# A tau-masked attention with a gated feed-forward layer on one core: weight pieces of 512 columns, ninth blocks turned in the scores' banks, short query tiles as float32 quarters, another planned order

## The chip, the cores and the metric

The kernel runs on one core of one Trainium2 chip. The metric is the time of one execution on the device, in microseconds (us). The kernel before takes 1004.27 us, the median of 3 runs between 1001.59 and 1005.19. All engine times come from one profiled execution.

## What is computed

The reference is attention with a cut on the scores, and a feed-forward layer whose gate is a convolution of three taps over the tokens:

```python
scores = scale * np.matmul(q, k.transpose(0, 1, 3, 2))          # batch 8, heads 8, 576 tokens, head size 64
thresh = np.max(scores, axis=-1, keepdims=True) - tau
scores = np.where(scores >= thresh, scores, -1000000000.0)
attn = softmax(scores)                                            # written out in the reference
x = np.matmul(attn, v)                                            # heads side by side: 8 x 576 x 512
h = np.maximum(x @ w_in, 0.0)                                     # 512 -> 1024
conv_out = sum over 3 taps of conv_w[k] * h shifted by one token
out = h / (1 + exp(-conv_out)) @ w_out                            # 1024 -> 512
```

Everything is float32 (the weights arrive as eight-byte floats, whose two words the kernel puts together itself).

## The kernel before

**Tiling.** Heads go in pairs, four pairs to a batch. The 576 queries of a batch are tiles of 128, 128, 128, 128 and 64. Each batch is cut in two chunks, tiles 0 and 1, and tiles 2, 3 and 4. One query tile of one head pair is a *unit*: 20 units to a batch, 160 in all.

**A unit.** TensorE (PE) makes the scores of one head, 128 queries by 576 keys, in two banks of PSUM, 288 columns in each (L423 in the first batch, L434 in the others). VectorE (DVE) takes the negated maximum of each row (L443), ScalarE (ACT) the exponent (L449), DVE masks by the threshold and sums (L452), GpSimd (POOL) normalises (L482). Then PE turns the result, 128 by 1152 for the two heads, in nine blocks of 128 by 128 (L504): groups of 4, 4 and 1 blocks, each in a bank of the pool `ps_t`, which has two banks, and ACT copies each group out (L498). When a pair's last tile of a chunk is turned, PE multiplies by the values (L550, `pa`, also in `ps_t`).

**Precision.** In the first batch the scores are plain float32 products in which a product of 64 rows fills half of PE, so two halves run side by side. In batches 1 to 7 q and k are split in a high and a low part (ACT and POOL, L369 to L391 and L253) and the scores are products of type float32r on all 128 rows. The last tile has 64 queries. In the first batch its two heads are four products in the quarters of PE. In the others they are eight float32r products of 288 columns: four for the second head, 128 queries wide (the upper half is what is wanted), and four for the first.

**Feed-forward.** For a chunk, eight blocks of w_in products (L580, `ph`), the rectifier on ACT (L595), three taps and the gate (POOL L598, DVE L607 and L614, ACT L616), a split (ACT L624, POOL L253), and per 128 tokens 24 products with w_out (L645, `po`). Weights are split too: `split` (L268 to L313) takes a piece of 256 columns in two buffers of the tag `ot`, by one load on SP's queue, ACT L279, DVE L283, L287, L291 and L295, ACT L298 and POOL L253. There are 32 such pieces.

**Order.** A planner (`Plan`, L50 to L191) places all operations before anything runs: each has an engine, a cost, the operations that it follows, and a rank (the unit that it belongs to less a lead from `AHEAD`). The planner walks through time and lets each free engine take the ready operation of the lowest rank. `WRATE` sets the ranks of the weight pieces, `KEEP` and `SWITCH` how long PE stays in one kind of product, `BACKLOG` and `ALT` when DVE takes work of POOL. Each engine then runs its list in that order. What waits for what on the chip is not the planner's: it is made from the tiles that each operation touches.

Of the kernel before, what the change touches and what calls it, by code (L numbers as in the profile page):

```python
# [18 lines left out]
AHEAD = {'s': 4.5, 't': 4.0, 'a': 3.5, 'prep': 5.5, 'w': 2.0}  # L19
# [4 lines left out]
BACKLOG = {'pool': 10000.0, 'dve': 500.0, 'act': 9e9}  # L24
WRATE = (1.75, 1.25)
ALT = 3.0
# [7 lines left out]
KEEP = 0.6  # L34


class Buf:
# [6 lines left out]
    def __getitem__(self, key):  # L44
        if self.tile is None:
            self.tile = self.pool.tile(self.shape, self.dtype, tag=self.tag, bufs=self.bufs, name=self.name)
        return self.tile[key]

# [146 lines left out]
def tile_tau_attention_gated_ffn(  # L195
# [3 lines left out]
    kd: bass.AP,  # L199
    vc: bass.AP,  # L200
# [19 lines left out]
    GROUPS = [(0, 1), (2, 3, 4)]  # L220
    CHUNKS = [(0, 255), (255, 321)]
    COLS = [(0, 256), (254, 322)]
    NEW = [(0, 256), (256, 320)]
# [4 lines left out]
    ps_s = ctx.enter_context(tc.tile_pool(name="ps_s", bufs=2, space=PSUM))  # L228
# [11 lines left out]
    op("sp", 100, lambda: nc.sync.dma_start(tau_sb[:], tau.broadcast_to([P, 1])), w=[(tau_sb, 0)], ahead=100.0)  # L240

# [26 lines left out]
    def split(src, n, name, high, low, hr, lr):  # L268


        tmp = plan.buf(wk, "ot", 2, [P, 3 * WN], U32, name)

        def view(dtype=F32):
            words = tmp[:, :2 * n].rearrange("p (f two) -> p f two", two=2)
            return [x.bitcast(dtype) for x in (words[:, :, 0], words[:, :, 1], tmp[:, 2 * n:3 * n])]

        def f1():
            lo, hi, a = view()
            nc.scalar.activation(a, hi, AF.Abs)  # L279

        def f2():
            a = view()[2]
            nc.vector.tensor_scalar(a, a, TINY, None, op0=ALU.max)  # L283

        def f3():
            a = view(U32)[2]
            nc.vector.tensor_scalar(a, a, 3, 0x3FFFFFF8, op0=ALU.logical_shift_left, op1=ALU.bitwise_and)  # L287

        def f4():
            lo, hi, a = view(U32)  # L290
            nc.vector.scalar_tensor_tensor(a, hi, 0xC0000000, a, op0=ALU.bitwise_and, op1=ALU.bitwise_or)  # L291

        def f5():
            lo, hi, a = view(U32)
            nc.vector.scalar_tensor_tensor(a, lo, 29, a, op0=ALU.logical_shift_right, op1=ALU.bitwise_or)  # L295

        def f6():
            nc.scalar.activation(high(), view()[2], AF.Copy)  # L298

        def f7(engine):  # L300
# [481 lines left out]
```

## Time and profile before

| | |
|---|---|
| runs | 1001.59, 1004.27, 1005.19 us |
| profiled execution | 1007.23 us, its span from first to last instruction 1005.4 us |
| granted TensorE clock, mean | 0.974 |
| busy: PE, DVE, ACT, POOL | 948.6, 816.0, 706.4, 725.6 us |
| instructions of PE, DVE, ACT, POOL | 6368, 2023, 1575, 1157 |
| moved by DMA | 77.76 MB, 77 GB/s on average |

Busy time of PE counts overlapping matmuls once. A matmul's row shows its whole passage, so the start of one and the start of the next tell what it takes in a stream. Idle time of an engine counts only where something waits for it.

### The profile page before, as it was taken

The numbers are of one execution on the slowest core, as the hardware profiler recorded it, in microseconds if no ns is written. First come the engines' busy times: TensorE is split into PE (matmuls) and PEld (weight loads), VectorE is DVE, ScalarE is ACT, GpSimd is POOL, SyncE is SP. The second block draws the span as 40 slices with busy tenths as digits, with TensorE's granted clock in tenths as the row PEclk, the third lists the DMA queues.
The fourth block names the chain that finished last, engine by engine and source line by source line (L and its number), as shares of the span: only waits on it lengthen the run. The fifth ranks groups of instructions, "written<-read, shape, count | busy, mean of one in ns | idle before, by whom it ended". The sixth has DMA issues, their size and how long they took to land.

```text
span 1005.4 us, 19531 instructions
## 1 busy us (share of the span) xinstructions
PE 948.6 (94%) x6368; PEld 769.7 (77%) x6368; DVE 816.0 (81%) x2023; ACT 706.4 (70%) x1575; POOL 725.6 (72%) x1157
## 2 busy tenths in 40 slices
PE   6788777999999999999999999999999999999998
PEld 3455455778888788878888888887788888887796
DVE  5889998887887967898788877898789877897543
ACT  5576676777777776777777777678776776776543
POOL 3567787687677978697776978698766886696433
PEclk9796997999999999999999999999999999999999
DMA  6434342223221233222312232213322121211000
GB/s 172 127 104 128 102 125 80 76 62 97 83 71 51 78 91 90 66 65 81 109 57 65 64 100 71 81 36 102 100 75 63 53 82 57 70 47 38 22 22 32
DMA packets 47172, 77.76 MB, mean 77 GB/s; under 512 B 5600, under 2 KB 23008, under 8 KB 47072
## 3 DMA queue, kind: packets, MB, share of 16 engines
q1 hardware_dynamic: 47072, 76.53, 26.0%
q8 instruction: 51, 0.84, 0.4%
q14 instruction: 49, 0.40, 0.1%
HBM read 67.07 MB, written 9.44 MB: 76 GB/s over the span
## 4 chain that ended last, share of the span: by engine, by line
PE 74%; DVE 8%; POOL 8%; issue 3%; ACT 3%; DMA 3%; SPq 1%; POOLq 0%; ACTq 0%; DVEq 0%
PE po L645 18%; PE ph L580 16%; PE ps_s L434 13%; PE pa L550 13%; PE ps_t L504 12%; POOL em L482 2%; POOL gl L253 2%; DVE few L443 2%; DVE em L452 2%; PE ps_s L423 1%; DMA stage<-in_w_out_dram 1%; DVE t L607 1%; POOL t L598 1%; ACT eT L498 1%; POOL ks L253 1%
## 5 line engine op out<-in xcount | busy, mean ns | idle before, releaser
L482 POOL TENSOR_SCALAR em<-em,few 128x576 f32<-128x576 f32 x288 | 259.6, 908 | 44.1 <-DVE few L477 30.5
L443 DVE TENSOR_REDUCE few<-ps_s 128x1 f32<-128x576 f32 x288 | 213.2, 750 | 67.2 <-PE ps_s L434 51.6
L580 PE MATMUL ph<-x,w1h 128*128 128x322 f32 (+1 forms) x1024 | 254.5, 311 | 1.3 <-ACT hp L595 1.0
L452 DVE SCALAR_TENSOR_TENSOR em<-ps_s,few,em 128x576 f32<-128x576 f32 x288 | 231.6, 810 | 28.6 <-ACT em L449 24.3
L449 ACT ACTIVATE em<-ps_s,few 128x576 f32<-128x576 f32 x288 | 211.8, 742 | 52.2 <-DVE few L443 43.7
L498 ACT ACTIVATE eT<-ps_t 128x512 f32<-128x512 f32 (+1 forms) x448 | 200.0, 479 | 53.7 <-PE ps_t L504 50.2
L504 PE MATMUL ps_t<-ident,em 128*128 128x128 f32 x1280 | 204.1, 282 | 18.9 <-POOL em L482 12.0
L504 PEld LDWEIGHTS ps_t<-ident,em 128*128 128x128 f32 x1280 | 154.5, 144 | 62.2 <-POOL em L482 30.1
L434 PE MATMUL ps_s<-ks,q 128*128 128x288 f32 (+1 forms) x1120 | 193.6, 307 | 6.0 <-DVE em L452 6.0
L607 DVE SCALAR_TENSOR_TENSOR t<-hp,cw,t 128x255 f32<-128x255 f32 (+1 forms) x256 | 172.7, 681 | 23.9 <-POOL t L598 20.1
L580 PEld LDWEIGHTS ph<-x,w1h 128*128 128x128 f32 x1024 | 180.1, 192 | 10.0 <-issue 3.5
L434 PEld LDWEIGHTS ps_s<-ks,q 128*128 128x128 f32 (+1 forms) x1120 | 161.1, 186 | 18.5 <-DVE em L452 6.8
L550 PE MATMUL pa<-eT,v 128*64 128x256 f32 (+1 forms) x1280 | 172.9, 417 | 1.0 <-ACT eT L498 1.0
L580 PE MATMUL ph<-x,w1l 128*128 128x322 f32 (+1 forms) x512 | 153.0, 299 | 0.1
L253 POOL TENSOR_TENSOR gl<-t,gh 128x321 fp32r<-128x321 f32 (+13 forms) x184 | 119.5, 659 | 36.0 <-ACT gh L624 33.8
L550 PEld LDWEIGHTS pa<-eT,v 128*64 128x64 f32 x1280 | 87.8, 139 | 69.8 <-issue 7.1
L645 PE MATMUL po<-w2h,gh 128*128 128x512 f32 x288 | 121.2, 421 | 2.5 <-ACT w2h L298 1.9
L645 PE MATMUL po<-w2l,gh 128*128 128x512 f32 x288 | 113.7, 395 | 0.8 <-POOL w2l L253 0.8
L645 PE MATMUL po<-w2h,gl 128*128 128x512 f32 x288 | 113.2, 393 | 0.4 <-POOL hp L590 0.3
L253 POOL TENSOR_TENSOR q<-xq,q 128x256 fp32r<-128x256 f32 (+1 forms) x112 | 93.9, 844 | 18.1 <-ACT q L391 16.8
L598 POOL TENSOR_SCALAR t<-hp,cw 128x321 f32<-128x321 f32 (+1 forms) x128 | 70.6, 553 | 45.6 <-ACT hp L595 40.5
L580 PEld LDWEIGHTS ph<-x,w1l 128*128 128x128 f32 x512 | 98.2, 192 | 0.9 <-POOL w1l L253 0.3
(54 smaller groups left out, 1115.8 us busy)
## 6 DMA issues: line engine op xcount, KB each, us to landing
v<-in_vc_dram SPq DMA_DIRECT2D x64, 320.0 KB, 2.9
out_dram<-ot SPq DMA_DIRECT2D x36, 256.0 KB, 2.1
xk<-in_kd_dram SPq DMA_DIRECT2D x28, 320.0 KB, 3.0
xq<-in_qd_dram SPq DMA_DIRECT2D x56, 160.0 KB, 2.2
xk<-in_kd_dram SPq DMA_DIRECT2D x28, 288.0 KB, 2.9
xq<-in_qd_dram SPq DMA_DIRECT2D x56, 128.0 KB, 2.1
stage<-in_w_in_dram SPq DMA_DIRECT2D x16, 256.0 KB, 3.1
stage<-in_w_out_dram SPq DMA_DIRECT2D x16, 256.0 KB, 2.6
```

Source lines behind the costliest of these rows:

```text
L253: engines[e].tensor_tensor(dst, x, y, op=ALU.subtract)
L434: nc.tensor.matmul(ps[:(r + 1) * n, c, :CH], lhsT=qt[j][i][:, o - r * n:o + n], rhs=kt[j][:, at:at + CH], start=(i == 0), stop=(i == 1))
L443: nc.vector.tensor_reduce(few[:rows, nm], ps[:rows, :, :CH], op=ALU.max, axis=mybir.AxisListType.XY, negate=True)
L449: nc.scalar.activation(view(), ps[:rows, :, :CH], AF.Exp, bias=few[:rows, nm])
L452: nc.vector.scalar_tensor_tensor(view(), ps[:rows, :, :CH], few[:rows, th], view(), op0=ALU.is_ge, op1=ALU.mult, accum_out=few[:rows, total])
L482: engines[e].tensor_scalar(sl, sl, few[:rows, 6 + h:7 + h], few[:rows, 8 + h:9 + h], op0=ALU.mult, op1=ALU.add)
L498: "act", act(w, True), lambda dst=dst, src=src: nc.scalar.activation(dst(), src(pt), AF.Copy),
L504: nc.tensor.transpose(out=pt[:, i * P:(i + 1) * P], in_=em[:, (b0 + i) * P:(b0 + i + 1) * P], identity=ident[:])
L550: nc.tensor.matmul(pa[j * D:(j + 1) * D, :w], lhsT=vt[:, blk + j, :], rhs=eT[:, blk, :w], start=(r == 0), stop=(r == 4))
L580: nc.tensor.matmul(ph[:, :an], lhsT=w1[w][:, cb, fs], rhs=xs[cb][:, h, :an], start=(cb == 0 and i == 0), stop=(cb == NCB - 1 and i == 2))
L607: nc.vector.scalar_tensor_tensor(t[:, :kn], hp[:, k:kn + k], cw[:, 3 * f + k:3 * f + k + 1], t[:, :kn], op0=ALU.mult, op1=ALU.add)
L645: nc.tensor.matmul(po[:], lhsT=x[:, f, at:at + P], rhs=w[:, f, :], start=(f == 0 and i == 0), stop=(f == NFB - 1 and i == 2))
```

## The change

It has five parts.

1. **Weights in pieces of 512 columns**: 16 pieces for 32. The step that was DVE L283 goes to POOL (new line L322, as minimum and maximum in one), DVE keeps three steps (L325, L328, L331). The raw words lie in the four buffers of the tag `ks`, which later hold the keys, the value in the two buffers of `q2`. The first three loads are issued by ACT's queue.
2. **Ninth blocks by the scores**: the ninth 128 by 128 block of a tile, and the 64-wide one of the last tile, are turned into columns 384 to 511 of a bank of the scores, of which these use 288. `ps_t` then holds groups of four blocks and `pa`. The two score buffers are now fixed tiles, used in turn.
3. **The last 64 queries**: in batches 1 to 7 too, they are four plain float32 products in quarters. For these, k comes once more as it is (`kp`), in a buffer of the tag `xk`, and 64 queries of q, scaled by ACT (L397). q and k lose their 64 extra columns (q pieces of 256 for 320, k of 576 for 640).
4. **First batch**: the scale goes to q instead of k, with one load for a pair's keys and one for its queries in place of four and two. A first exponent on one column (L267) loads ACT's table early.
5. **Order**: other leads and thresholds, and the first chunk's w_out block comes in its own feed-forward part (`EARLY`).

```diff
-AHEAD = {'s': 4.5, 't': 4.0, 'a': 3.5, 'prep': 5.5, 'w': 2.0}
+AHEAD = {'s': 6.0, 't': 3.5, 'a': 3.5, 'prep': 5.0, 'w': 2.0, 'load': 2.25}
-BACKLOG = {'pool': 10000.0, 'dve': 500.0, 'act': 9e9}
-WRATE = (1.75, 1.25)
-ALT = 3.0
+BACKLOG = {'pool': 19600.0, 'dve': 500.0, 'act': 9000000000.0}
+WRATE = (1.238, 0.731)
+ALT = 1.47
...
-        tmp = plan.buf(wk, "ot", 2, [P, 3 * WN], U32, name)
+        stage = plan.buf(wk, "ks", 4, [P, 2, S], U32, name)
+        value = plan.buf(wk, "q2", 2, [P, 2, 2 * P], U32, f"{name}_f")
...
-        op("dve", dve(n / 2), f2, w=[a], ahead=w)
+        op("pool", n * 1.69 + 80, f1, w=[a], ahead=w, other=[("dve", 150 + n * 0.65)])
...
-    WN = 256
+    WN = 512
...
+    scores = [plan.buf(ps_s, f"ps_s{i}", 1, [P, 2, 512], F32, f"ps_s{i}") for i in range(2)]
...
+            if not j:
+                q1, q2 = (plan.buf(wk, f"q{x}", 2, [P, 2, QW], F32R, f"q{x}_{i}") for x in (1, 2))
+                whole[i] = (whole[i - NP][0] if o else plan.buf(wk, "ks", 4, [P, 2, S], F32R, f"ks_{b}_{p}"), q1, q2)
+            if not o:
+                prep_k(b, p, j, whole[i][0])
+            prep_q(i, b, p, j, *whole[i][1:])
+            if j and w % P:
+                last[i] = (*prep_rows(i, b, p, o + w - w % P, w % P, "q"), None)
...
-            pt = plan.buf(ps_t, "ps_t", 2, [P, 512], F32, f"ps_t_{u}_{i}")
             width = sum(w for w, _, _ in evacs)
+            if width > P:
+                pt = plan.buf(ps_t, "ps_t", 2, [P, 512], F32, f"ps_t_{u}_{i}")
+                part, bank = (pt, 0), lambda: pt
+            else:
+                at = turns("t", 4)
+                pt, half = scores[at % 2], at // 2
+                part, bank = (pt, 1 + half), lambda: pt[:, half, 512 - P:]
```

New function of the plain scores' operands, called for batch 0 and for each last tile:

```python
def prep_rows(i, b, p, o, w, tag):
    k = plan.buf(wk, "xk", 2, [P, S + D], F32, f"k_{i}")
    q = plan.buf(wk, tag, 2, [P, 2, w], F32, f"{tag}_{i}")
    a = AHEAD["prep"]
    op("sp", 450, lambda: nc.sync.dma_start(k[:], kp[b, p]), w=[(k, 0)], ahead=a + 2)
    op("sp", 450, lambda: nc.sync.dma_start(q[:], qd[b, p, :, :, o:o + w]), w=[(q, 0)], ahead=a + 2)
    op("act", act(2 * w), lambda: nc.scalar.activation(q[:], q[:], AF.Copy, scale=0.125), w=[(q, 0)], ahead=a)
    return k, q
```

**PE at a last tile.** Before, in batch 4, third pair (`ps_s_0_7355` holds the scores of the 64 queries of both heads):

```order
L434 MATMUL ps_s_1_7347<-ks_2_1_5699,q_4_2_1_1_7014 128x288
L434 MATMUL ps_s_1_7347<-ks_2_1_5699,q_4_2_1_1_6961 128x288
L434 MATMUL ps_s_1_7347<-ks_2_1_5699,q_4_2_1_1_7014 128x288
L434 MATMUL ps_s_0_7355<-ks_2_1_5699,q_4_2_1_1_6961 128x288
L434 MATMUL ps_s_0_7355<-ks_2_1_5699,q_4_2_1_1_7014 128x288
L434 MATMUL ps_s_0_7355<-ks_2_1_5699,q_4_2_1_1_6961 128x288
L434 MATMUL ps_s_0_7355<-ks_2_1_5699,q_4_2_1_1_7014 128x288
L434 MATMUL ps_s_0_7355<-ks_2_0_5672,q_4_2_0_1_6902 64x288
L434 MATMUL ps_s_0_7355<-ks_2_0_5672,q_4_2_0_1_6918 64x288
L434 MATMUL ps_s_0_7355<-ks_2_0_5672,q_4_2_0_1_6902 64x288
L434 MATMUL ps_s_0_7355<-ks_2_0_5672,q_4_2_0_1_6918 64x288
L504 MATMUL ps_t_4_7370<-ident,em_7223 128x128 x4
```

Now, at a last tile of the same batch:

```order
L606 MATMUL ph_3_6367<-x_5044,w1h 128x322
L577 MATMUL pa_6372<-eT_6252,v_6054 64x256 x10
L450 MATMUL ps_s_108<-k_5988,q_5354 64x288 x4
L531 MATMUL ps_t_0_6406<-ident,em_6224 128x128 x4
L531 MATMUL ps_t_4_6417<-ident,em_6224 128x128 x4
L531 MATMUL ps_s_115<-ident,em_6347 128x128
L457 MATMUL ps_s_115<-ks_1_5667,q_37_6208 128x288
```

Eight float32r products have become four plain ones, and here they stand behind the product with the values, which also runs in halves of PE. The ninth block goes to `ps_s_115`, the second score buffer, just ahead of that buffer's next scores.

**PE at a ninth block.** Now, in batch 3, with what each row waits for (the name is an engine's semaphore):

```order
L457 MATMUL ps_s_115<-ks_0_2462,q_20_3123 128x288 [waits DVE_49]
L457 MATMUL ps_s_115<-ks_0_2462,q_20_3146 128x288
L457 MATMUL ps_s_115<-ks_0_2462,q_20_3123 128x288
L457 MATMUL ps_s_115<-ks_0_2462,q_20_3146 128x288
L531 MATMUL ps_t_4_3343<-ident,em_3169 128x128 [waits Activation_49,Pool_49]
L531 MATMUL ps_t_4_3343<-ident,em_3169 128x128 x3
L531 MATMUL ps_s_115<-ident,em_3169 128x128 [waits DVE_49]
```

The scores of one unit are written to the second buffer, and four blocks later the ninth block of another unit goes into the same buffer. It waits for DVE: the semaphore's value is that of the row maximum of the scores just written. Before, such a block went to a bank of `ps_t`, and waited for ACT's copy out of that bank.

**DVE at a weight piece.** Before, two pieces of 256 columns side by side (`stage_400`, `stage_415`):

```order
L283 TENSOR_SCALAR stage_400<-stage_400 128x256
L446 TENSOR_SCALAR few_395<-few_395,tau_sb 128x1
L287 TENSOR_SCALAR stage_400<-stage_400 128x256
L443 TENSOR_REDUCE few_458<-ps_s_0_448 128x1
L291 SCALAR_TENSOR_TENSOR stage_400<-stage_400 128x256
L283 TENSOR_SCALAR stage_415<-stage_415 128x256
L295 SCALAR_TENSOR_TENSOR stage_400<-stage_400 128x256
L287 TENSOR_SCALAR stage_415<-stage_415 128x256
```

Now, one piece of 512 (`stage_120` holds the words, `stage_f` the value):

```order
L325 TENSOR_SCALAR stage_f<-stage_f 128x512
L468 TENSOR_SCALAR few_329<-few_329,tau_sb 128x1
L328 SCALAR_TENSOR_TENSOR stage_f<-stage_120,stage_f 128x512
L474 SCALAR_TENSOR_TENSOR em_344,few_329<-ps_s_115,few_329,em_344 128x576
L331 SCALAR_TENSOR_TENSOR stage_f<-stage_120,stage_f 128x512
```

Three DVE steps now do what eight did. The last piece's last step stands behind 37 row maxima in DVE's list, where it stood behind 48.

More of the change, by code (lines that the diff above doesn't have):

```diff
@@ L47, in __getitem__ @@
         return self.tile[key]
+Chunk = collections.namedtuple("Chunk", "b tiles new cols tokens done")
 class Plan:
@@ L289, in f4 @@
         def f4():
[L290 to L300, printed above, removed]
-            subtract(engine, low(), view()[2], high().bitcast(F32))
-        lo, hi, a = ((tmp, i) for i in range(3))
@@ L660, in ffn @@
         if c < len(chunks):
[L661 to L664 removed]
+            first = [(chunks[c].cols[1] * 5, lambda f=f: mm1(c, f, xs[c])) for f in range(NFB)]
+        done = [chunks[i].done if i >= 0 else 0 for i in (c - 2 + (c - 1 < EARLY), c - 1 + (c < EARLY))]
+        second = [(5120, lambda m=m: mm2(m)) for m in range(*done)]
         seq = []
         n1, n2 = MOE
+        if c < EARLY:
+            return first + second
         while first or second:
```

254 lines of the change are left out of this document (128 added, 126 removed).

## The prediction

> **What bounds the kernel now.** I read the stages first (busy time of each engine in four stretches), then the slices of the page, then the waits of PE, then the groups.
>
> ```profile
> 0.00:178.00 178.00, 132.97 (x757) 85.51 (x757) 152.35 (x389) 117.25 (x260) 117.02 (x182) 0.86 0.41 120
> 200.00:950.00 750.00, 743.36 (x5173) 622.67 (x5172) 623.99 (x1552) 552.96 (x1230) 572.77 (x909) 1.00 0.24 71
> 950.00:1005.40 55.40, 51.30 (x286) 43.70 (x284) 21.92 (x37) 20.06 (x52) 20.59 (x42) 1.00 0.08 29
> ```
>
> The columns are length, busy PE, its weight loads, DVE, ACT, POOL, granted clock, DMA share, GB/s. There are two regimes. From 200 to 950 us PE is busy for 743.4 of 750 us at full clock, and DVE for 624 (83%): PE's work sets the pace, and whatever PE is spared or made to wait for reaches the end. From 0 to 178 us it is otherwise: PE is idle for 45 us and has a clock of 0.86 on the mean, while DVE, at 152 of 178 us, is the fullest engine.
>
> ```profile
> PE   6788777999999999999999999999999999999998
> DVE  5889998887887967898788877898789877897543
> PEclk9796997999999999999999999999999999999999
> ```
>
> Slices are 25.1 us. DVE is at 8 or 9 tenths from the second to the sixth, just where PE is at 7 or 8 and its clock falls to 6 and 7 tenths: a hungry PE. The first stretch ends with the last weight piece (its last DVE step, L295, starts at 177.3 us).
>
> ```profile
> L295 DVE SCALAR_TENSOR_TENSOR stage<-stage x32: 407/421/1755, 22.8 to 177.3; 128x256 uint32<-128x256 uint32 x32
> DVE few L443 <- PE ps_s L423: 14.5, 11, 7.5
> PE ps_t L504 <- POOL em L482: 3.5, 6, 1.6
> PE ps_t L504 <- DVE x L561: 1.1, 1, 1.1
> PE ps_s L434 <- DVE em L452: 0.8, 2, 0.6
> ```
>
> The second row is DVE's largest wait up to 178 us: 14.5 us, of which 7.5 are the wait for the first scores. So behind that start DVE is nearly without a break. The last three rows are what PE waited for between 200 and 980 us: under 6 us in the largest three groups. There is almost nothing to gain there, and much to lose.
>
> **The change part by part.**
>
> *The last 64 queries (PE).* Rows of the timeline of PE, start and length in us: eight float32r products in the steady part, then the four quarters (eight instructions) in the first batch.
>
> ```profile
> 222.17 1.22 PE L434 MATMUL ps_s<-ks,q 128*128 128x288 f32 x8
> 223.23 0.28 PE L580 MATMUL ph<-x,w1h 128*128 128x256 f32 x1
> ...
> 104.44 0.28 PE L580 MATMUL ph<-x,w1l 128*128 128x256 f32 x1
> 104.56 0.28 PE L580 MATMUL ph<-x,w1h 128*128 128x256 f32 x1
> 104.76 0.72 PE L423 MATMUL ps_s<-ks,q 64*64 64x288 f32 x8
> 105.41 0.77 PE L504 MATMUL ps_t<-ident,em 128*128 128x128 f32 x5
> 105.93 0.36 PE L580 MATMUL ph<-x,w1h 128*128 128x256 f32 x1
> ```
>
> Eight products take 1.06 us from start to start. The quarters take 0.65 us, but entering costs: the product ahead of them holds PE for 0.20 us instead of 0.12, and the first instruction behind them is some 0.05 to 0.10 us longer. That makes 0.79 to 0.84 us standing alone. There are 28 such tiles (7 batches, 4 pairs): 28 x 1.06 = 29.7 us go, 28 x 0.84 = 23.5 come. By PE's list, products that run in halves or quarters stand directly beside the product with the values at 34 places where they did at 9, so some 25 boundaries of about 0.15 us are shared: 3.8 us less. Sum: 29.7 - 23.5 + 3.8, **10 us less PE work**. Bounds: 6 (nothing shared) and 11 (all at 0.79). All of it lies in the stretch that PE bounds, so it counts in full.
>
> *Weight pieces of 512 (start).*
>
> ```profile
> L295 DVE SCALAR_TENSOR_TENSOR stage<-stage 128x256 uint32<-128x256 uint32 x32 | 18.8, 591 | 0.0
> L291 DVE SCALAR_TENSOR_TENSOR stage<-stage 128x256 uint32<-128x256 uint32 x32 | 17.2, 539 | 0.0
> L283 DVE TENSOR_SCALAR stage<-stage 128x256 f32<-128x256 f32 x32 | 14.2, 445 | 4.8 <-ACT stage L279 4.8
> L287 DVE TENSOR_SCALAR stage<-stage 128x256 uint32<-128x256 uint32 x32 | 13.5, 425 | 0.0
> L607 DVE SCALAR_TENSOR_TENSOR t<-hp,cw,t 128x321 f32<-128x321 f32 x128 | 91.2, 721 | 13.4 <-POOL t L598 11.8 <-POOL hp L590 0.9 <-POOL hp L592 0.4
> L607 DVE SCALAR_TENSOR_TENSOR t<-hp,cw,t 128x255 f32<-128x255 f32 x128 | 81.5, 640 | 10.4 <-POOL t L598 8.3 <-POOL hp L590 1.7
> L598 POOL TENSOR_SCALAR t<-hp,cw 128x321 f32<-128x321 f32 x64 | 37.5, 587 | 24.2 <-ACT hp L595 21.1 <-PE ps_s L434 1.6
> ```
>
> Per piece DVE spends 591 + 539 + 445 + 425 ns = 2.00 us, 64 us for 32. No row has 512 columns. The two forms of L607 differ by 81 ns for 66 columns, 1.23 ns a column; so 256 more columns add 0.31 us, and three steps take 0.90 + 0.85 + 0.74 = 2.49 us. If a piece simply took double, it would be 1.18 + 1.08 + 0.85 = 3.11 us. For 16 pieces that is 40 or 50 us against 64: DVE is spared 14 to 24 us, and more if the short steps grow less than the long ones. I take **22**, near the upper end: the median of L295 (421 ns) lies far below its mean, so much of a short piece's time is waiting that comes with every instruction. DVE is the fullest engine of the stretch, so I let it pass to the end one to one; below, it could be 0 (another engine takes over), above, 28. POOL takes the sixteen new steps (at the 587 ns of L598 for 321 columns, about 0.8 us each, 13 us) and loses 16 of 32 subtractions' fixed part; with 117 of 178 us busy it has room. The new first loads, the early table load and the scale on q shift the first scores by less than 1 us, at nothing.
>
> *Ninth blocks by the scores (PE waits).* This adds waits. In PE's list 110 of the 160 ninth blocks wait for an operation that reads the scores in the buffer where the block goes: 46 for the maximum, 30 for the exponent, 34 for the mask. The planner does not count these waits. Behind the block on PE stands everything else, since PE works in order. One set of scores in the steady part:
>
> ```profile
> 236.39 1.84 PE L434 MATMUL ps_s<-ks,q 128*128 128x288 f32 x12
> 238.07 0.60 PE L504 MATMUL ps_t<-ident,em 128*128 128x128 f32 x4
> ...
> 238.27 0.76 DVE L443 TENSOR_REDUCE few<-ps_s 128x1 f32<-128x576 f32 x1 [0.21 <-PE ps_s L434]
> 239.40 0.75 ACT L449 ACTIVATE em<-ps_s,few 128x576 f32<-128x576 f32 x1
> 240.39 0.80 DVE L452 SCALAR_TENSOR_TENSOR em<-ps_s,few,em 128x576 f32<-128x576 f32 x1
> ```
>
> PE is free of the scores at 238.07; the maximum is read until 239.03, the exponent until 240.15, the mask until 241.19: 1.0, 2.1 and 3.1 us later. Of the 46 blocks that wait for the maximum, 16 stand only about 0.5 us of PE work behind the scores, 13 about 1.0, the rest later. The first sixteen then wait 0.5 us even when DVE is prompt: 8 us. Of the thirty, five stand under 1.5 us behind (0.6 us each, 3 us); of the thirty-four, seven under 2.9 (0.4 us each, 3 us). That is 14 us with prompt readers. The upper end is half a reader for every one of the 110, 110 x 0.38 = 42 us; below, 5 us, since blocks in the start cost PE nothing that it lacks. I take **15**: DVE and ACT are idle for 17% and 26% of the steady part, so readers are mostly prompt.
>
> The Trainium skill, "PSUM — Partial Sum Buffer", section "PSUM bank collisions raise a hardware error", says that any two engines on the same bank and quadrant collide, whatever the columns, reads included, and that semaphores must keep them apart by bank. No run here shows a collision; what the list of waits shows agrees with the rule, and by it the waits above cannot be planned away while block and scores share a bank. It is the mechanism of the second rival.
>
> *The rest, at nothing.* Extra loads (28 times 320 KB of keys and 64 KB of queries, less the columns dropped: some 8 MB on 77.8) find DMA at 24%. The keys for a last tile share the two buffers `xk` with the next batch's keys; the load of a second head's keys then waits for the last tile's scores. It takes 2.9 us, then 684 + 680 ns on ACT and 1.5 us on POOL, at seven batch boundaries:
>
> ```profile
> L253 POOL TENSOR_TENSOR ks<-xk,ks 64x576 fp32r<-64x576 f32 x28 | 41.1, 1469 | 2.3
> L369 ACT ACTIVATE xk<-xk 128x576 f32<-128x576 f32 x28 | 19.1, 684 | 8.0 <-DMA xk<-in_kd_dram 6.2 <-POOL few L474 1.0 <-POOL em L482 0.7
> L370 ACT ACTIVATE ks<-xk 128x576 fp32r<-128x576 f32 x28 | 19.0, 680 | 0.0
> xk<-in_kd_dram SPq DMA_DIRECT2D x28, 288.0 KB, 2.9
> ```
>
> Feed-forward products of the chunk before hide it, a chunk's worth of which is queued; without that cover it costs at most 7 x 5.8 = 41 us, and 0 is the nearer end. `ps_t` serves two groups per unit instead of three; PE lost 4.6 us there in the two groups shown first, so a gain is at most 5 us. With fewer columns POOL and ACT save about as much as the new q scale costs.
>
> **Sum.** -10 - 22 + 15 = -17 us. The profiled execution took 1007.2 us with a span of 1005.4, 3 us over the median of the runs, so the sum is set against the median: 1004 - 17 = **987 us**.
>
> **Rivals.**
>
> *The shared banks cost more than everything else brings.* The waits come to 42 us, and DVE's maxima, 71 of which now wait for ACT's copy of a ninth block, hold up the rest a little: 1004 - 10 - 22 + 42 + 6 = 1020 us. For it: 110 waits in the list of an engine that has no slack. Against: the steady part's DVE and ACT have slack. It decides from 32 us on, a mean of 0.2 us for each of the 160 blocks.
>
> *The start does not shorten.* A piece passes ACT, POOL, DVE, ACT and POOL, two values at a time; if that chain sets the pace and not DVE's sum, the start keeps its length: 1004 - 10 + 15 - 4 = 1005 us. For it: POOL is now in the chain twice, with steps of 908 ns of L482 ahead of it. Against: 152 of 178 us of DVE.
>
> ```profile
> L482 POOL TENSOR_SCALAR em<-em,few 128x576 f32<-128x576 f32 x288 | 259.6, 908 | 44.1 <-DVE few L477 30.5
> ```
>
> *The waits are over when PE comes.* If PE lags behind its plan everywhere in the steady part, readers are done: 1004 - 10 - 22 = 972 us.
>
> *The quarters bring nothing.* If each block pays its entry and exit twice over, 10 us fall away: 997 us. The rows at 104.76 speak against it.
>
> [...]
>
> **How the numbers follow.** Forecast 987 us: 0.43. Banks, 1020: 0.25. Start unchanged, 1005: 0.12. Waits over, 972: 0.17. Quarters in vain, 997: 0.03. A measurement of this kernel tells about 0.5% from no change, 5 us, so faster means under 999: 0.43 + 0.17 + 0.03 = 0.63, of which the 997 us, hardly beyond the bound, give 0.01 to the middle: 0.62. With the unchanged start's 0.12 the middle has 0.13. Slower: 0.25. The range ends below where the fast case has the ends of its terms (1004 - 11 - 28 - 5 for `ps_t`: 960) and above just over the banks' 1020, where it leaves out the dearest part of that case: 960 to 1022.
>
> **What would show it.** Right: the last weight piece's DVE step ends near 150 us or earlier, the quarters at about 0.65 us, PE's steady waits grow by some 15 us with ninth blocks named, behind L465, L471 and L474. Wrong: those waits at 40 us or more, PE under 95% busy in the steady part, or weights that end near 178 us still.

## The result, and the profile after

| | before | changed |
|---|---|---|
| runs | 1004.71 us, median of 5 (1001.59 to 1007.02) | 1013.07 us, median of 5 (1012.69 to 1015.16) |
| ratio | 1 | 1.0092, 95% interval 1.0078 to 1.0107 |
| span of the profiled execution | 1005.4 us | 1010.9 us |
| granted clock, mean | 0.974 | 0.98 |

The changed kernel is **slower by 0.9%**, some 9 us, where 987 us were forecast. The time lies inside the range, but the kernel moved the other way than forecast, towards the first rival (the shared banks). The same stages as before, in the changed kernel (length, then busy PE, its weight loads, DVE, ACT, POOL, clock, DMA share, GB/s):

```profile
0.00:178.00 178.00, 135.54 (x810) 89.01 (x811) 137.01 (x323) 114.89 (x233) 144.32 (x182) 0.88 0.40 125
200.00:950.00 750.00, 728.02 (x5092) 590.22 (x5090) 616.43 (x1502) 547.41 (x1247) 565.23 (x930) 1.00 0.27 82
950.00:1010.90 60.90, 56.80 (x312) 47.77 (x309) 23.46 (x40) 21.73 (x56) 21.21 (x43) 1.00 0.07 27
```

In the steady part PE is idle for 22.0 of 750 us, where it was idle for 6.6. In the start DVE has 137 us for 152, but POOL has 144 for 117 and is now the fullest engine there. The slices of the page (25.3 us each) say where:

```profile
PE   5868788999999999999999999999999999999998
DVE  4877798888988878787788878897787887997343
POOL 3888998975887678787786768786786777886343
PEclk9878799999999999999999999999999999999999
```

From the second to the seventh slice POOL stands at 8 and 9 tenths, and PE still at 6 to 8. What PE waited for from 200 to 950 us, first in the changed kernel (`ps_s L531` is a ninth block in a bank of the scores, `L555` the 64-wide one, `L457` the scores):

```profile
PE ps_s L531 <- DVE em L474: 4.7, 7, 1.1
PE ps_s L531 <- DVE few L465: 4.1, 7, 0.8
PE ps_s L555 <- DVE few L465: 3.3, 6, 0.6
PE ps_s L457 <- DVE em L474: 1.7, 4, 0.6
PE ps_s L457 <- ACT eT L525: 1.4, 3, 0.9
```

Blocks wait for DVE's mask and maximum, and scores wait for ACT's copy of a block. Neither stood in the list of before. One such place in the steady part, PE first, then DVE:

```profile
637.67 0.69 PE L457 MATMUL ps_s<-ks,q 128*128 128x288 f32 x4
638.20 0.60 PE L531 MATMUL ps_t<-ident,em 128*128 128x128 f32 x4
639.89 0.44 PE L531 MATMUL ps_s<-ident,em 128*128 128x128 f32 x2 [1.10 <-DVE em L474]
640.09 0.77 PE L457 MATMUL ps_s<-ks,q 128*128 128x288 f32 x4
640.70 0.39 PE L671 MATMUL po<-w2h,gh 128*128 128x512 f32 x1
```

```profile
638.24 0.21 DVE L468 TENSOR_SCALAR few<-few,tau_sb 128x1 f32<-128x1 f32 x1
639.01 0.82 DVE L474 SCALAR_TENSOR_TENSOR em<-ps_s,few,em 128x576 f32<-128x576 f32 x1 [0.56 <-ACT em L471]
```

The block could start at about 638.7. The mask of the scores in its bank runs until 639.83, since DVE itself had waited for ACT's exponent; PE stands for 1.10 us, and all that is behind the block stands with it, the w_out product at 640.70 too. DVE is idle for 0.56 us just before: here the reader wasn't busy with other things, it was late by its own chain. That is the rarer kind. Of the 24 waits of such blocks for DVE that the profile lists in the steady part, DVE was idle just before the reader in four; in the others it came straight from another operation. Often that was the other maximum, when two sets of scores had come close together (PE, then DVE):

```profile
303.42 1.22 PE L457 MATMUL ps_s<-ks,q 128*128 128x288 f32 x8
304.47 0.60 PE L531 MATMUL ps_t<-ident,em 128*128 128x128 f32 x4
305.62 0.44 PE L531 MATMUL ps_s<-ident,em 128*128 128x128 f32 x2 [0.55 <-DVE few L465]
```

```profile
304.14 1.42 DVE L465 TENSOR_REDUCE few<-ps_s 128x1 f32<-128x576 f32 x2 [2.66 <-PE ps_s L457]
```

DVE stood idle for 2.66 us, then had two maxima at once, and the block waits 0.55 us for the second. In eight of the thirteen waits for a maximum DVE had come straight from another maximum.

The pieces and the quarters, by line (min, median and max of a duration, first and last start):

```profile
L322 POOL TENSOR_SCALAR stage_f<-stage_f x16: 1914/1993/2432, 13.1 to 131.8; 128x512 f32<-128x512 f32 x16
L328 DVE SCALAR_TENSOR_TENSOR stage_f<-stage,stage_f x16: 671/691/1781, 22.6 to 139.1; 128x512 uint32<-128x512 uint32 x16
L331 DVE SCALAR_TENSOR_TENSOR stage_f<-stage,stage_f x16: 670/684/1183, 24.9 to 143.1; 128x512 uint32<-128x512 uint32 x16
```

```profile
226.41 0.72 PE L450 MATMUL ps_s<-k,q 64*64 64x288 f32 x8
227.06 0.66 PE L531 MATMUL ps_t<-ident,em 128*128 128x128 f32 x4
```

The last weight step starts at 143 us, 34 us earlier than before, and the quarters take 0.65 us from start to start, both as the prediction had them. The new step on POOL takes 2.0 us, not 0.8.

**A count of what PE loses.** A matmul that waits at the head of the stream can still be shown as busy, so idle time is too small a measure. I count each instruction of PE at the distance of starts that its kind has in an unbroken stream (133 ns for scores, 150 and 120 for the w_in products of a second and a first chunk, 230 for those with w_out, 109 for a turned block, 589 for a set of quarters, with 0.09 to 0.2 us where the shape changes). The rest of the time is lost. These costs are my estimates from the traces; in the first 200 us the loss also holds what a lower clock takes (granted there 0.87 before, 0.90 in the changed kernel, 0.95 in e3), so a few us between two kernels in that column need not be waits. For all kernels of this study:

| kernel | time, us | ratio to before | PE work | lost, 0 to 200 us | lost, 200 to 950 us |
|---|---|---|---|---|---|
| before | 1004.7 | 1 | 907.5 | 79.2 | 14.0 |
| changed | 1013.1 | 1.0092 | 896.6 | 72.8 | 36.6 |
| e1, floor on DVE | 1009.4 | 1.0058 | 897.9 | 70.7 | 33.9 |
| e2, ninth blocks in `ps_t` | 980.4 | 0.9763 | 897.9 | 67.0 | 9.0 |
| e3, floor without the minimum | 1007.9 | 1.0044 | 896.6 | 68.4 | 35.6 |
| e4, leads of before | 1036.5 | 1.0330 | 900.8 | 78.2 | 49.7 |
| e5, e1 and e2 | 975.9 | 0.9733 | 897.7 | 63.0 | 9.1 |
| e6, before with quarters | 1015.9 | 1.0132 | 900.9 | 78.6 | 29.9 |
| e7, before with ninth blocks by the scores | 1036.5 | 1.0334 | 907.7 | 81.4 | 40.1 |
| e8, before with the new leads | 999.5 | 0.9950 | 906.8 | 76.0 | 13.9 |
| e9, e2 with pieces of 256 | 989.5 | 0.9866 | 898.1 | 79.0 | 7.6 |
| e10, before with quarters and new leads | 987.2 | 0.9825 | 897.6 | 72.3 | 11.4 |
| e11, e2 with a cheap floor | 970.3 | 0.9658 | 897.9 | 56.4 | 8.4 |
| e12, e2 with the true price of the floor | 978.5 | 0.9744 | 897.4 | 67.5 | 8.5 |

For the change as a whole: 10.9 us less work, 6.4 us less lost in the start, 22.6 us more lost in the steady part, 0.2 us at the end: 5.5 us, the difference of the two spans. The medians lie 8.4 us apart, since the profiled execution of before was itself 2.5 us over its median.

### The profile page after: what moved, and what is told of

Same layout as the page of the kernel before. It is cut to its first block, busy times and chain, and to the rows that moved or that the text cites. A ratio compares the mean times of both kernels' runs of the same rounds, so it can differ in the third digit from the quotient of the medians.

```text
span 1010.9 us, 19416 instructions
## 1 busy us (share of the span) xinstructions
PE 941.8 (93%) x6368; PEld 744.7 (74%) x6368; DVE 797.2 (79%) x1913; ACT 700.8 (69%) x1572; POOL 751.9 (74%) x1188
## 4 chain that ended last, share of the span: by engine, by line
PE 61%; POOL 14%; DVE 13%; ACT 6%; issue 4%; DMA 1%; SPq 0%; POOLq 0%; ACTq 0%; DVEq 0%
PE ph L606 15%; PE po L671 15%; PE pa L577 10%; PE ps_t L531 8%; PE ps_s L457 8%; POOL em L503 5%; DVE few L465 5%; DVE em L474 4%; PE ps_s L450 3%; DVE t L633 2%; ACT em L471 2%; PE ps_s L531 2%; POOL gl L280 2%; ACT eT L525 2%; POOL stage_f L322 2%
## 5 line engine op out<-in xcount | busy, mean ns | idle before, releaser
L503 POOL TENSOR_SCALAR em<-em,few 128x576 f32<-128x576 f32 x288 | 262.7, 920 | 30.6 <-DVE few L498 22.8
L606 PE MATMUL ph<-x,w1h 128*128 128x322 f32 (+1 forms) x1024 | 248.8, 308 | 0.4 <-ACT ot L678 0.3
L525 ACT ACTIVATE eT<-ps_t 128x512 f32<-128x512 f32 x288 | 168.8, 599 | 37.0 <-PE ps_t L531 35.7
L633 DVE SCALAR_TENSOR_TENSOR t<-hp,cw,t 128x255 f32<-128x255 f32 (+1 forms) x256 | 177.1, 695 | 20.0 <-POOL t L624 17.9
L531 PE MATMUL ps_t<-ident,em 128*128 128x128 f32 x1152 | 173.2, 281 | 20.7 <-POOL em L503 18.5
L531 PEld LDWEIGHTS ps_t<-ident,em 128*128 128x128 f32 x1152 | 135.3, 143 | 54.0 <-POOL em L503 29.4
L457 PE MATMUL ps_s<-ks,q 128*128 128x288 f32 x896 | 160.5, 305 | 7.0 <-DVE em L474 2.9
L457 PEld LDWEIGHTS ps_s<-ks,q 128*128 128x128 f32 x896 | 131.4, 189 | 25.9 <-issue 5.2
L280 POOL TENSOR_TENSOR gl<-t,gh 128x321 fp32r<-128x321 f32 (+13 forms) x184 | 119.4, 662 | 14.5 <-ACT gh L650 12.7
L671 PE MATMUL po<-w2h,gh 128*128 128x512 f32 x288 | 118.7, 412 | 0.0
L280 POOL TENSOR_TENSOR ks<-xk,ks 64x576 fp32r<-64x576 f32 x56 | 80.7, 1440 | 12.8 <-ACT ks L406 8.9
```

The costliest lines, as they stand in the source:

```text
L280: engines[e].tensor_tensor(dst, x, y, op=ALU.subtract)
L457: nc.tensor.matmul(ps[:, c, :CH], lhsT=q[:, h, o:o + n], rhs=k[:, h, c * CH:(c + 1) * CH], start=(i == 0), stop=(i == 1))
L503: engines[e].tensor_scalar(sl, sl, few[:rows, 6 + h:7 + h], few[:rows, 8 + h:9 + h], op0=ALU.mult, op1=ALU.add)
L525: "act", act(w, True), lambda dst=dst, src=src: nc.scalar.activation(dst(), src(bank()), AF.Copy),
L531: nc.tensor.transpose(out=pt[:, i * P:(i + 1) * P], in_=em[:, (b0 + i) * P:(b0 + i + 1) * P], identity=ident[:])
L606: nc.tensor.matmul(ph[:, :an], lhsT=w1[w][:, cb, fs], rhs=xs[cb][:, h, :an], start=(cb == 0 and i == 0), stop=(cb == NCB - 1 and i == 2))
```

## The experiments

The theory after the result: ninth blocks in the scores' banks cost PE some 22 us, and the start stays long because the new step fills POOL. Against it stand the new leads as the cause, and a start bound by something else. Each kernel below is the changed kernel (e1 to e5, e9, e11, e12) or the kernel before (e6, e7, e8, e10) with the edit shown; the planner orders anew in each.

### e1: the floor of a weight piece on DVE

```diff
-        op("pool", n * 1.69 + 80, f1, w=[a], ahead=w, other=[("dve", 150 + n * 0.65)])
+        op("dve", 150 + n * 0.55, lambda: f1("dve"), w=[a], ahead=w)
```

> The changed kernel with one step of a weight piece, the floor of L322 (maximum and minimum), put back from POOL to DVE; the planner is told DVE's cost. Theory POOL: the sixteen floors of 2.09 us (33.5 us in all) fill POOL in the start and hold PE there. With POOL relieved the start gives back what the prediction had expected of it beyond the 6 us it gave: 1013 - 15 = 998 us, and PE's loss in the first 200 us falls from 73 to some 58 us; DVE takes sixteen steps of about 0.7 us. Rival chain: the length of the chain of steps of a piece bounds the start; then a shorter floor changes the time by under 4 us. Rival DVE: DVE is the fullest again, and the time rises to 1020.

Measured: 1009.44 us, ratio 1.0058 (1.0039 to 1.0076), 3.6 us less than the changed kernel. The start in this kernel:

```profile
0.00:178.00 178.00, 136.85 (x816) 88.55 (x817) 147.61 (x341) 116.17 (x235) 119.15 (x168) 0.89 0.39 125
```

```profile
L322 DVE TENSOR_SCALAR stage_f<-stage_f x16: 407/478/1519, 22.0 to 135.0; 128x512 f32<-128x512 f32 x16
```

POOL is relieved (119 us for 144) and PE hardly gains (136.9 for 135.5). A floor takes DVE 0.48 us (median) for POOL's 2.0, but DVE is at 148 us, the fullest again, as the rival on DVE had it, though the time didn't rise. My expectation of 15 us fell: that POOL alone bounds the start is wrong. The 3.6 us lie within what the rival on the chain of steps allowed; e5 and e11 together speak against that one (under e11).

### e2: the ninth blocks back in ps_t

```diff
-            if width > P:
-                pt = plan.buf(ps_t, "ps_t", 2, [P, 512], F32, f"ps_t_{u}_{i}")
-                part, bank = (pt, 0), lambda: pt
-            else:
-                at = turns("t", 4)
-                pt, half = scores[at % 2], at // 2
-                part, bank = (pt, 1 + half), lambda: pt[:, half, 512 - P:]
+            pt = plan.buf(ps_t, "ps_t", 2, [P, 512], F32, f"ps_t_{u}_{i}")
+            part, bank = (pt, 0), lambda: pt
```

> The changed kernel with the ninth blocks back in the two banks of ps_t, nothing else edited (the planner orders anew). Theory banks: ninth blocks by the scores lost some 22 us more of PE's time between 200 and 950 us than the three groups in ps_t lost before; the time falls to 1013 - 22 = 991 us, and PE's waits of L531 there fall to about 6 us. Rival order: the steady losses come of the new leads; the time stays within 5 us of 1013, the waits only move to ps_t.

Measured: 980.38 us, ratio 0.9763 (0.9738 to 0.9788). That is 33 us less than the changed kernel (1.0092 - 0.9763 of 1004 us), more than expected. The steady part, and the three largest of PE's waits in it:

```profile
200.00:950.00 750.00, 746.68 (x5256) 611.91 (x5255) 615.48 (x1498) 550.66 (x1267) 573.33 (x964) 1.00 0.28 83
```

```profile
PE ps_t L526 <- DVE x L583: 0.7, 1, 0.7
PE po L666 <- POOL gl L280: 0.4, 1, 0.4
PE ps_t L526 <- DVE few L498: 0.4, 1, 0.4
```

PE is idle for 3.3 us of 750 where it was for 22.0. By the count of losses 27.6 us come back in the steady part: 17.5 at blocks of 128 (26.6 lost before them for 9.1), 4.0 at the 64-wide ones, 6.2 at scores. Another 5.8 come back in the start. So the blocks by the scores are the cause of the loss, with 33 us; their two banks in `ps_t` would have been enough.

The Trainium skill, "PSUM — Partial Sum Buffer", section "PSUM bank collisions raise a hardware error", has it that two engines must be kept apart by bank and quadrant even where their columns differ. The trace agrees as far as it goes: the block at 639.89 lies in columns 384 to 511 and the mask reads columns below 288 of each bank, and the block still waits for the mask. The wait is for a semaphore of the program; what the chip would do without it no run here shows.

### e3: the floor as a maximum alone

```diff
-            engines[e].tensor_scalar(v(), v(), TINY, HUGE, op0=ALU.max, op1=ALU.min)
+            engines[e].tensor_scalar(v(), v(), TINY, None, op0=ALU.max)
```

> The changed kernel with L322 as a maximum alone, without the minimum, still on POOL. Theory: the pair of operations is what makes a 512-column step take 2.09 us where L503 takes 0.92 for 576; alone it takes about 1.0 us, POOL is spared 17 us and the time falls by 6 to 10 us, to about 1005. Rival: a maximum is slow on POOL by itself; the step stays at 2 us and the time at 1013.

Measured: 1007.94 us, ratio 1.0044 (1.0025 to 1.0062).

```profile
L322 POOL TENSOR_SCALAR stage_f<-stage_f x16: 1497/1712/2002, 13.4 to 126.7; 128x512 f32<-128x512 f32 x16
```

The minimum costs 0.28 us of 1.99 (medians). It is the maximum that is slow, as the rival said, though the time does fall by 5 us, a little less than the theory expected from a larger saving.

### e4: the leads of before in the changed kernel

```diff
-AHEAD = {'s': 6.0, 't': 3.5, 'a': 3.5, 'prep': 5.0, 'w': 2.0, 'load': 2.25}
-BACKLOG = {'pool': 19600.0, 'dve': 500.0, 'act': 9000000000.0}
-WRATE = (1.238, 0.731)
-ALT = 1.47
+AHEAD = {'s': 4.5, 't': 4.0, 'a': 3.5, 'prep': 5.5, 'w': 2.0, 'load': 2.0}
+BACKLOG = {'pool': 10000.0, 'dve': 500.0, 'act': 9e9}
+WRATE = (1.75, 1.25)
+ALT = 3.0
...
-EARLY = 1
+EARLY = 0
...
-KEEP = 0.84
+KEEP = 0.6
```

> The changed kernel with the leads and thresholds of before (AHEAD, BACKLOG, WRATE, ALT, KEEP, EARLY), the rest of the change kept. Theory POOL and banks: the numbers of the order matter little; the time is within 8 us of 1013. Rival order: the new numbers themselves cost, and with the old ones the time falls to 995 or less.

Measured: 1036.52 us, ratio 1.0330 (1.0307 to 1.0352). Both expectations missed, on the same side: the new numbers don't cost, they save 23 us here. With the old ones 49.7 us are lost in the steady part for 36.6, 78.2 in the start for 72.8, and PE's work is 4 us more. The order is a term of its own, which the prediction had put at nothing. But these are the old numbers and not quite the old order: `WRATE` is in pieces per unit, and a piece is now twice as long, so 1.75 asks for the weights at twice the pace of before. They end early:

```profile
L331 DVE SCALAR_TENSOR_TENSOR stage_f<-stage,stage_f x16: 675/692/1634, 23.4 to 114.0; 128x512 uint32<-128x512 uint32 x16
```

The last such step starts at 114 us, where it starts at 143 with the new numbers. How much of the 23 us that makes isn't separated.

### e5: both edits, e1 and e2

> The changed kernel with both edits: ninth blocks in ps_t and the floor of a weight piece on DVE. Theory: the two costs lie in different places and add: 980.4 - 4 = 976 us. Rival: the waits at shared banks hid what DVE and POOL gain in the start; without them the floor on DVE brings the whole 12 to 15 us that POOL is relieved of: 967 us. Rival in the other direction: DVE, not held up by banks any more, is the fullest engine of the start, and one more step per piece on it costs: 985 us.

Measured: 975.94 us, ratio 0.9733 (0.9704 to 0.9763). The two add, 33 and some 4 us (3 by the ratios, and the interval overlaps that of e2), as two costs in different places would. It is the fastest kernel here that computes everything, 2.7% under before. The start:

```profile
0.00:178.00 178.00, 139.94 (x874) 93.23 (x875) 152.22 (x357) 122.02 (x248) 130.00 (x183) 0.92 0.41 128
```

DVE stands at 152 us of 178 once more, as it did before the change: with POOL relieved, DVE is the fullest engine again.

### e6: the quarters alone, in the kernel before

```diff
+                if kq is not None:
+                    for r, j in enumerate(js):
+                        for c in range(2):
+                            on = slice(c * D, (c + 1) * D)
+                            at = j * CH + r * D
+                            nc.tensor.matmul(
+                                ps[r * n:(r + 1) * n, c, :CH], lhsT=kq[1][on, j, :n], rhs=kq[0][on, at:at + CH],
+                                start=True, stop=True
+                            )
+                    return
...
+        if j and g and not plain(b):
+            last[i] = prep_rows(i, b, p, 4 * P, S - 4 * P)
```

The function `prep_rows` is that of the change; q and k lose their 64 further columns.

> The kernel before with the last tiles of batches 1 to 7 alone changed: four plain float32 products in quarters, their own keys and queries loaded and scaled, q and k without their 64 extra columns. Theory: PE is the bound there and saves 10 us: 994 us. Rival: the further loads and the shared buffers xk hold PE up at batch boundaries, and the gain is lost: 1002 us or more.

Measured: 1015.92 us, ratio 1.0132 (1.0096 to 1.0169): slower by 13 us. PE's work falls by 6.6 us, but 29.9 us are lost in the steady part for 14.0. The largest waits there:

```profile
PE ps_t L525 <- POOL em L503: 8.3, 14, 1.7
PE ps_s L455 <- DVE em L473: 4.2, 6, 1.3
```

PE waits for POOL's normalising (L503 is L482 of before) and for a score buffer, not for the new loads or for `k` and `q` of the last tile. So the rival's place is wrong as well.

### e7: the ninth blocks by the scores alone, in the kernel before

```diff
-            ps = plan.buf(ps_s, "ps_s", 2, [P, 2, 512], F32, f"ps_s_{u}_{h}")
+            ps = scores[turns("s", 2)]
...
-            pt = plan.buf(ps_t, "ps_t", 2, [P, 512], F32, f"ps_t_{u}_{i}")
+            if width > P:
+                pt = plan.buf(ps_t, "ps_t", 2, [P, 512], F32, f"ps_t_{u}_{i}")
+                part, bank = (pt, 0), lambda: pt
+            else:
+                at = turns("t", 4)
+                pt, half = scores[at % 2], at // 2
+                part, bank = (pt, 1 + half), lambda: pt[:, half, 512 - P:]
```

> The kernel before with the ninth blocks alone put by the scores, in before's leads. Theory banks: it costs at least what it cost in the changed kernel, 33 us, and with a shorter lead of the scores over the blocks (0.5 units for 2.5) more: 1035 to 1050 us. Rival: the cost came of the changed kernel's long lead, and with before's leads it is under 15 us: below 1020.

Measured: 1036.47 us, ratio 1.0334 (1.0300 to 1.0368). The step costs 33 us in this kernel too, under other leads and with nothing else of the change: shown from both sides. That also speaks against the new order that the planner makes for each kernel as the cause, since the two pairs were ordered with different numbers. The extra cost that I expected of a shorter lead didn't come.

### e8: the new leads alone, in the kernel before

```diff
-AHEAD = {'s': 4.5, 't': 4.0, 'a': 3.5, 'prep': 5.5, 'w': 2.0}
+AHEAD = {'s': 6.0, 't': 3.5, 'a': 3.5, 'prep': 5.0, 'w': 2.0}
...
-BACKLOG = {'pool': 10000.0, 'dve': 500.0, 'act': 9e9}
-WRATE = (1.75, 1.25)
-ALT = 3.0
+BACKLOG = {'pool': 19600.0, 'dve': 500.0, 'act': 9e9}
+WRATE = (2.476, 1.462)
+ALT = 1.47
...
-KEEP = 0.6
+KEEP = 0.84
```

> The kernel before with the changed kernel's leads and thresholds alone (AHEAD, BACKLOG, ALT, KEEP, and WRATE doubled, since pieces are half as long). Theory lead: a longer lead of the scores over the blocks (2.5 units for 0.5) has the results of POOL's normalising ready before PE turns them; PE's loss between 200 and 950 us falls from 14 to under 10 us, and the time by 4 to 10 us, to 994 to 1000. Rival: the numbers fit only the changed kernel; the time stays or rises, 1004 or more.

Measured: 999.48 us, ratio 0.9950 (0.9928 to 0.9971), 5 us less. The size came as expected, the place didn't. PE no longer waits for POOL's normalising in the steady part (3.5 us before), but it waits 3.2 us for another step of POOL ahead of the products with w_out: 13.9 us are lost in the steady part, as good as before, and of the 4.0 us between the two spans 3.2 are in the start (76.0 lost for 79.2) and 0.7 in PE's work. The ten runs lie between 995.76 and 1004.61 us and the profiled one, 1003.33, is among the slower, so this is the account of a smaller gain than the median's.

### e9: pieces of 256 columns, with the ninth blocks in ps_t

The kernel is e2 with this edit.

```diff
-WRATE = (1.238, 0.731)
+WRATE = (2.476, 1.462)
...
-    WN = 512
+    WN = 256
...
-            src[c * P:(c + 1) * P, f], WN, f"stage_{i}", h, l, *((x, (c, f.start)) for x in dst), "act" if i < 3 else "sp"
+            src[c * P:(c + 1) * P, f], WN, f"stage_{i}", h, l, *((x, (c, f.start)) for x in dst), "act" if i < 6 else "sp"
```

> The kernel with the ninth blocks back in ps_t, and besides weight pieces of 256 columns in place of 512 (32 pieces, ranks twice as dense, the first six loads on ACT's queue). Theory: the length of a piece counts by the fixed part of each of DVE's and ACT's steps; DVE has some 15 us more to do in the start, and the time rises by 8 to 15 us, to 988 to 995. Rival: the start isn't DVE's to set, and the time stays within 4 us of 980.

Measured: 989.49 us, ratio 0.9866 (0.9838 to 0.9894), 9 us more than e2, which has 512. All of it is in the start (79.0 us lost for 67.0).

```profile
L328 DVE SCALAR_TENSOR_TENSOR stage_f<-stage,stage_f x32: 407/424/951, 21.1 to 153.9; 128x256 uint32<-128x256 uint32 x32
```

A step of 256 columns takes 424 ns, one of 512 takes 691: 267 ns for the further 256. If the first 256 cost the same, 157 of the 424 ns come with every instruction (an estimate from these two lengths).

### e10: quarters and new leads, in the kernel before

The edits of e6 and e8 together.

> The last run but one of the quarters alone, with the changed kernel's leads and thresholds as well. Theory lead: the 13 us that the quarters alone cost come of the short lead of before (0.5 units), under which shorter scores reach PE's turns ahead of POOL; with the long lead the quarters bring what they save PE, some 7 to 10 us under the run of the order alone, and the steady loss is under 12 us. Rival: the quarters themselves bring a wait, of the shared buffers xk or of q; then the steady loss stays near 30 us, and the time over 1005.

Measured: 987.24 us, ratio 0.9825 (0.9797 to 0.9852): 12.2 us less than e8. The steady loss is 11.4 us, and the waits that e6 showed have shrunk:

```profile
PE ps_t L525 <- ACT eT L519: 2.1, 3, 1.5
PE ps_s L455 <- DVE em L473: 1.4, 2, 0.7
```

The wait for POOL's normalising is gone from the list. So the quarters bring what the prediction said, and a little more, under the new order. With the order of before, the same saving on PE turned into waits. That the new numbers do it is shown; which of the five settings does, the lead of the scores or another, isn't.

### e11: the floor as two multiplications by one

```diff
-            engines[e].tensor_scalar(v(), v(), TINY, HUGE, op0=ALU.max, op1=ALU.min)
+            engines[e].tensor_scalar(v(), v(), 1.0, 1.0, op0=ALU.mult, op1=ALU.mult)
```

The kernel is e2 with this edit; it leaves out the floor that lifts the smallest values.

> The kernel with the ninth blocks in ps_t, and L322 on POOL as two multiplications by 1 in place of maximum and minimum; it leaves out the floor that lifts the weights' smallest values. Theory: it is maximum and minimum that POOL takes long for; the step falls from 2.0 to 0.85 us, as a step of L503 per column, POOL is spared 18 us in the start and the time falls by 4 to 10 us from 980. Rival: a 512-column step in place costs 2 us whatever the operation; nothing changes.

Measured: 970.29 us, ratio 0.9658 (0.9638 to 0.9679), 10 us less than e2.

```profile
L322 POOL TENSOR_SCALAR stage_f<-stage_f x16: 619/642/1143, 13.0 to 120.6; 128x512 f32<-128x512 f32 x16
```

The same tile, in place, on the same engine takes 0.64 us for 1.99: it is the operation. With POOL spared some 22 us and DVE not charged for it, the start loses 56.4 us for 67.0. So POOL's floor does cost 10 us, and putting it on DVE (e5) brings only some 4 of them, where DVE has 152 us of 178 to do. That also answers the rival on the chain: in e5 the chain is the shorter one (the floor takes 0.42 us, median, and stays on the engine of the next step; here 0.64), and yet e11 is 6 us faster. What the engines have to do counts here, more than the length of the chain.

### e12: the planner told the price of the floor

```diff
-        op("pool", n * 1.69 + 80, f1, w=[a], ahead=w, other=[("dve", 150 + n * 0.65)])
+        op("pool", n * 3.9 + 80, f1, w=[a], ahead=w, other=[("dve", 150 + n * 0.65)])
```

The kernel is e2 with this edit.

> The kernel with the ninth blocks in ps_t, where the planner is told 2.08 us for L322 in place of 0.95. Theory: a wrong price upsets the order in the start; told the right one the planner gives some of these steps to DVE and orders the rest better, 974 to 978 us. Rival: the order is robust against it, 980 us.

Measured: 978.53 us, ratio 0.9744 (0.9717 to 0.9770); e2 has 0.9763. The intervals overlap, and the start loses as much (67.5 for 67.0). All sixteen steps stayed on POOL, so the theory's shift to DVE wasn't tried. The order isn't upset by the wrong price; it is the 2 us that cost, as e11 shows.

## Why the prediction was wrong, step by step

By ratios times 1004 us, along e8, e10, e2 and the changed kernel, the change falls into four parts:

| part | forecast | measured |
|---|---|---|
| order (e8) | 0 | -5 |
| quarters (e10 against e8) | -10 | -12.5 |
| the rest: pieces, POOL's floor, first batch, `EARLY` (e2 against e10) | -22 | -6 |
| ninth blocks by the scores (changed against e2) | +15 | +33 |
| sum | -17 | +9 |

Two terms of the sum were mis-sized, the ninth blocks (33 us for 15) and the weight pieces (6 us for 22), and with these two the forecast of a faster kernel fell.

**The quarters** were right in their mechanism and, under the new leads, about right in size. But "all of it lies in the stretch that PE bounds, so it counts in full" holds only as long as nothing is late next. In the kernel before, with its order, it became a loss of 13 us (e6).

**The weight pieces.** One failed step is the sentence that POOL takes the sixteen new steps "at the 587 ns of L598 for 321 columns, about 0.8 us each, 13 us". The duration was taken from a row of another operation, two multiplications; a maximum with a minimum takes 2.09 us on the mean, 33.5 us in all. The groups of the first 178 us:

```profile
L322 POOL TENSOR_SCALAR stage_f<-stage_f 128x512 f32<-128x512 f32 x16 | 33.5, 2091 | 5.1 <-ACT stage_f L319 4.3 <-DVE few L468 0.3
L328 DVE SCALAR_TENSOR_TENSOR stage_f<-stage,stage_f 128x512 uint32<-128x512 uint32 x16 | 14.8, 927 | 0.0
L331 DVE SCALAR_TENSOR_TENSOR stage_f<-stage,stage_f 128x512 uint32<-128x512 uint32 x16 | 12.0, 750 | 0.0
L325 DVE TENSOR_SCALAR stage_f<-stage_f 128x512 uint32<-128x512 uint32 x16 | 8.0, 502 | 3.2 <-POOL stage_f L322 3.2
```

DVE was spared even more than I said: eight of its steps became three and one of POOL's, and the three sum to 34.8 us for the 64 of before, 29 us and not 22. The second failed step is that I let this pass to the end one to one. Windows of 50 us in the start of the changed kernel show what took over:

```profile
50.00:100.00 50.00, 36.81 (x221) 23.82 (x218) 37.29 (x88) 29.36 (x57) 43.74 (x47) 0.80 0.45 142
100.00:150.00 50.00, 40.56 (x238) 24.93 (x238) 42.30 (x95) 33.54 (x74) 46.52 (x59) 0.86 0.20 62
```

POOL is busy for 44 and 47 of 50 us, DVE for 37 and 42. The case was a rival, "the start does not shorten", with a chain as its reason. The reason was another: two engines share the start's load, and what one is spared the other had been given. With a cheap step on POOL the start does pay: e11 loses 56.4 us where before loses 79.2, and the row above would read -17 for -22 (0.9658 against 0.9825). So some 10 of the 16 us that failed to come are the price of the floor. The last 5 stay open. The length of a piece by itself is worth about 10 us (e2 against e9).

**The ninth blocks** cost 33 us for 15. The mechanism, the waits for readers of the same bank, was right, and the rival of the shared banks (the first in the list, though the prediction also calls it the second) had named the point from which it decides, 32 us. The step that failed is the price, and by the count of e2 it failed in three places. The blocks themselves lose 21.5 us more in the steady part than in `ps_t`, for 15: I let readers be "mostly prompt" because DVE is idle for 17% of that part, but the work comes to DVE in bunches, as at 304.14, or late by its own chain, as at 639.01, so an idle share doesn't make a reader prompt. The scores lose 6 us more, for which the sum had no term: they wait for readers too, by the list for DVE's mask (1.7 us) and for ACT's copy of a block (1.4). And I put the start at nothing for these blocks; 6 us were lost there too, as DVE also waits there for blocks in the scores' banks (DVE's waits in the first 178 us):

```profile
DVE few L465 <- PE ps_s L531: 5.4, 3, 2.1
DVE em L474 <- PE ps_s L531: 3.9, 3, 2.4
DVE few L465 <- ACT eT L525: 3.4, 4, 1.7
```

These three groups make 12.7 us of the 41 us that DVE is idle there. With the blocks back in `ps_t` (e2) none of the three is left in DVE's list: part of what DVE was spared had turned into waits on the shared banks.

**The order** was left at nothing, since only its rows and no price were read. It is worth 5 us by itself, 23 us in the changed kernel (e4, with the faster weights named there), and some 30 us in the kernel before when the quarters are in (e6 against e10).

**Signs to look for.** All three signs of being right were seen: the weights' end near 143 us, the quarters' 0.65 us, and PE's steady idle time, which grew by 15.4 us with ninth blocks named. None of the signs of being wrong was: PE is still busy for 97% of the steady part. So the signs could not tell the two outcomes apart. An early end of the weights says nothing on what PE could do in between, and idle time shows 15.4 us where the count of starts finds 22.6.

## What to carry to other kernels

Take the duration of an operation that moves to another engine from a row of that very operation there, or keep both ends of a wide range: the same tile takes 0.48 us on DVE and 0.64 or 1.99 us on POOL, by the operation. In this kernel a bank that is read in three steps (maximum, exponent, mask) stays taken until the last of them ends, whatever columns are free in it, and each such wait on PE holds up everything behind it: 33 us for 160 blocks. A saving on the engine that sets the pace needs an order that keeps its inputs early: the quarters cost 13 us under one and brought 12 under another, so try a saving with more than one order before it is judged.

## What was not expected of the hardware

On POOL, 512 columns of float32 in place take 642 ns with two multiplications, 1712 ns with a maximum and 1993 ns with a maximum and a minimum (medians of 16, e11, e3 and the changed kernel). The Trainium skill, "GPSIMD Engine Reference", section "4.1 Engine selection", puts operations with one input at roughly line rate on this engine, and lists the maximum among its elementwise examples. The multiplications come near that, with 1.25 ns a column, all told, beside the 1.04 ns for each further column of a step of DVE (e9); the maximum, with 3.3 ns a column, doesn't, and the measurement decides.

DVE does the same maximum and minimum in 478 ns (median, e1), less than the 684 to 691 ns of its two steps that read two tensors of as many columns (the changed kernel).
